# A decode block on one core: the loose rows of a weight matrix dealt anew to the transfer engines

## The chip, the cores and the metric

The kernel runs on one core of one Trainium2 chip. Times are microseconds of the device; the time of a kernel is the median of its runs. In the profile PE is the matrix engine (TensorE), PEld its weight load, DVE the vector engine, ACT the scalar engine, POOL is GpSimd, and SP (SyncE) computes nothing and issues transfers. The core's transfers (DMA) run on 16 transfer engines, numbered from 0.

## The reference

One decode step of a transformer block with adaptive layer norm, for two sequences (B = 2), one token each, width 512, all in float32:

```
mod = (silu(c) @ w_mod).reshape(2, 6, 1, 512)      # w_mod: 512 x 3072
sa, ca, ga, sb, cb, gb = mod[:, 0..5]
h = layernorm(x) * (1 + ca) + sa
q = (h @ wq) in 32 heads of 128                     # wq: 512 x 4096
p = softmax(q . k_cache * 128**-0.5)                # k_cache: 2 x 32 x 4096 x 128
x = x + ga * ((p . v_cache) @ wo)                   # wo: 4096 x 512
h = layernorm(x) * (1 + cb) + sb
f = h @ w1 + b1                                     # w1: 512 x 1376
x = x + gb * ((f * tanh(softplus(f))) @ w2)         # w2: 1376 x 512
```

K and V are 134 MB each. The last sixth of `w_mod` (columns 2560 to 3071) gives the gate gb; the change is about how its 512 rows are loaded.

## The kernel before

All inputs are laid out on the host into the order in which they are loaded. 36 loads (`stream`, L37) fill three buffers ("rooms" of 128 partitions x 64 KB) in turn; a load is issued when everything in the room three loads before has been used (`used`, L161). Loads 1 to 31 are one transfer each, of one head's K and parts of V, `wq` and `wo`. The last four are different:

- load 32: V of head 28, the last two blocks of `wo`, and the modulation's third part (`m2`);
- load 33: two transfers of 4 MB with V of heads 29 and 30;
- load 34: V of the last head, the modulation's fifth part (`m4`), and loose rows of its sixth;
- load 35: the fourth part (`m3`), `w1`, most of the sixth part (`m5`), `w2`, in seven transfers, the last with 512 columns of `w2`.

A head's K is multiplied with the query and summed on DVE (`products`, `sums`), the row maximum goes over PE (`row_max`), ACT takes the exponent (`soft_max`), PE multiplies with V (`weighted_v`). After the last head comes a tail in which PE leads: the output projection, the second layer norm, `w1`, the activation, `w2`, and the store. Matmuls named `busy` (L312, on `e` and `ident`) do work that nobody needs and keep PE occupied between steps.

**The sixth part of the modulation.** 512 rows are 384 in three blocks of 128 (`m5`), 32 that sit in an unused corner of a `w2` block, and 96 loose ones. Before, the loose ones are 4 x 20 rows (`m5p`: 20 partitions, four pieces of 512 columns side by side, so 20 rows of 8 KB) and 16 rows (`m5q`: 16 partitions of 2 KB). A tensor with fewer than 128 rows is issued by `load` as four transfers (L155), every fourth row each: `m5q` as four of four rows, `m5p` as four of five rows. The gate's matmuls (`modulation_5`, L534) take the loose pieces first (terms 0 to 4), then `m5`, then the corner.

**What sets the order.** The schedule is written by hand: an engine does its instructions in the order of the program. SyncE's queue is the list of loads. Each transfer tells of its end on one of eight semaphores (DMAHW0 to DMAHW7) which are taken in turn, so a transfer also waits, at its issue, until the one that used its semaphore eight transfers before has landed. Transfers of one queue are worked off in order on each of the 16 transfer engines; a transfer over 128 partitions uses all of them, eight rows each.

Of the kernel before, what the change touches and what calls it, by code (L numbers as in the profile page):

```python
# [8 lines left out]
F32 = mybir.dt.float32  # L9
# [4 lines left out]
P = 128  # L14
WIDTHS = (384, 384, 352, 256)
CHUNKS = [(g, j) for j in range(3) for g in range(4) if WIDTHS[g] > P * j]
STEP = 4
PIECES = (20, 20, 20, 20, 16)
WHOLE = PIECES.count(PIECES[0])
M5 = 3  # L20
REST0 = WIDTHS[2] - 2 * P
REST = 512 - P * M5 - sum(PIECES)
# [4 lines left out]
HALF = BIG // 2  # L27
SIZES = {
    "k": BIG, "v": HALF, "wq": W, "wo": W, "m01": 2 * W, "m2": W, "m3": W, "m4": W, "m5": 512 * M5,
    "m5p": 512 * WHOLE, "m5q": 512, "w1": 4 * sum(WIDTHS), "w2": 512 * len(CHUNKS),  # L30
}
OUT_STEP = 1
AHEAD = (14, 22)
# [3 lines left out]
def stream():  # L37


    order, n_v = [], 0  # L40
    for h in range(1, HEADS):
        order.append(("k", h))
        if h % HC == HC - 1 and HC < h < HEADS - 1:
            c = (h + 1) // HC
            order.append([("wq", c), ("wo", c - 2)])
        if h not in AHEAD:
            order += [("v", n_v, 0), ("v", n_v, 1)]
            n_v += 1
    order = [x if isinstance(x, list) else [x] for x in order]

    def size(x):
        return sum(SIZES[key[0]] for key in x)

    loads = [[([("m01", 0), ("wq", 0), ("wq", 1)], (4 * W,)), ([("k", 0)], (BIG,))]]
    for _ in range(1, HEADS):
        row = []
        while size(row) < ROW:
            room = ROW - size(row)
            row += order.pop(next(i for i, x in enumerate(order) if size(x) <= room))
        loads.append([(row, (ROW,))])  # L60
    last = [("v", h, i) for h in range(HEADS - 4, HEADS) for i in range(2)]
    assert order == [[key] for key in last[:2]], order
    loads += [
        [(last[:2] + [("wo", 6), ("wo", 7), ("m2", 0)], (BIG + 3 * W,))],
        [(last[2:4], (BIG,)), (last[4:6], (BIG,))],
        [([("m5q", 0)], (512,)), ([("m4", 0)] + last[6:], (W + HALF, W, W)), ([("m5p", 0)], (512 * WHOLE,))],
        [
            ([("m3", 0), ("w1", 0)], (W + 2 * sum(WIDTHS), 2 * sum(WIDTHS))),
            ([("m5", 0), ("w2", 0)], (512 * (M5 + 1), 5 * 512, 3 * 512, 512, 512)),
        ],  # L70
    ]
    return loads
# [3 lines left out]
def kernel(  # L76
# [48 lines left out]
    def take(t, keys):  # L125
        lo = 0
        for key in keys:
            kind, n = key[:2]
            part = t[:, lo : lo + SIZES[kind]]
            lo += SIZES[kind]  # L130
            if kind == "k":
                k_t[n] = part.rearrange("p (j d) -> p j d", d=DH)
            elif kind == "v":
                v_t[n, key[2]] = part.rearrange("p (c n) -> p c n", n=512)
            elif kind in ("wq", "wo"):
                (wq_t if kind == "wq" else wo_t)[n] = part.rearrange("p (k n) -> p k n", k=G)
            else:
                w_t[kind] = part.rearrange("p (k n) -> p k n", k={"w2": NCH, "m5": M5, "m5p": WHOLE, "m5q": 1}.get(kind, G))

    w_t = {}  # L140
    done = set()
# [1 line left out]
    def load(n):  # L143

        t = kvp.tile([P, ROW], F32, tag="room", name=f"room{n}", bufs=3)
        lo = 0
        for keys, srcs in loads[n]:
            take(t[:, lo:], keys)
            for src in srcs:
                rows, width = src.shape  # L150
                dst = t[:rows, lo : lo + width]
                if rows == P:
                    nc.sync.dma_start(out=dst, in_=src)
                else:
                    for i in range(STEP):  # L155
                        nc.sync.dma_start(out=dst[i::STEP], in_=src[i::STEP])
                lo += width

    loaded = 0

# [42 lines left out]
    for b in range(B):  # L203
        nc.vector.memset(same[PB * b : PB * (b + 1), b, :], 1.0)
    same = same.rearrange("p b r -> p (b r)")
    eps_t = const.tile([P, 48], F32, name="eps_t")
    nc.vector.memset(eps_t, EPS)

    ct = const.tile([P, G, R], F32, name="ct")
# [316 lines left out]
    w1_t, w2_t = w_t["w1"], w_t["w2"]  # L526
    gps = ov[1 - N % 2][:, :P]
    rest5 = slice(REST0, REST0 + REST)
    wm5p = [w_t["m5p"][:, n, :] for n in range(WHOLE)] + [w_t["m5q"][:, 0, :]]
    terms5 = [(ct5[:rows, n, :], wm5p[n][:rows]) for n, rows in enumerate(PIECES)]  # L530
    terms5 += [(ct[:, k, :], wm5[:, k, :]) for k in range(M5)]
    terms5.append((ct5[rest5, len(PIECES), :], w2_t[rest5, 0, :]))

# [28 lines left out]
    h2ps = columns(hq, "h2ps")  # L562
    nc.vector.tensor_copy(h2t[:, :, ::TB], h2ps)

    busy(1)
    modulation_5(4, len(PIECES))
    hq_pad = work.tile([P, 512], F32, tag="o", name="hq_pad")
    nc.gpsimd.memset(hq_pad[:, : NJ * P], 0.0)
    w1ps = wide_ps("w1ps")
# [61 lines left out]
def _lay_out(np, a):  # L631
# [21 lines left out]
    m5 = a["w_mod"][:, 512 * 5 :]  # L653
    m5p, f0 = np.zeros((P, len(PIECES) + 1, 512), m5.dtype), P * M5
    for n, size in enumerate(PIECES + (REST,)):
        to = REST0 if n == len(PIECES) else 0
        b1c[to : to + size, 12 + 2 * n : 14 + 2 * n] = a["c"].reshape(2, 512)[:, f0 : f0 + size].T
        m5p[to : to + size, n] = m5[f0 : f0 + size]
        f0 += size
    w2 = np.zeros((P, len(CHUNKS), 512), a["B_w2"].dtype)  # L660
    for n, (g, j) in enumerate(CHUNKS):
# [3 lines left out]
        w2[: f1 - f0, (n + 1) % len(CHUNKS)] = a["B_w2"][f0:f1]  # L665
    w2[REST0 : REST0 + REST, 0] = m5p[REST0 : REST0 + REST, -1]

    pieces = {**kv, "wq": wq, "wo": wo, "m01": [wm[:, :, :1024]], "w1": [w1], "w2": [w2], "m5p": [m5p[:, :WHOLE]], "m5q": [m5p[:, WHOLE]], "m5": [rows(m5)[:, :M5]]}
    for n in (2, 3, 4):
        pieces[f"m{n}"] = [wm[:, :, 512 * n : 512 * (n + 1)]]  # L670
    def piece(kind, n, part=None):
        row = pieces[kind][n].reshape(P, -1)
        return row if part is None else row[:, HALF * part : HALF * (part + 1)]

    loose = {"m5p": PIECES[0], "m5q": PIECES[-1]}
    arrays = {
        "head": np.stack([q_rows(a["c"]), q_rows(a["A_x"])], axis=1),
        "b1c": b1c,
# [36 lines left out]
```

## Time and profile before

| | |
|---|---|
| median of three runs | 695.11 us (695.01 to 695.4) |
| profiled execution | 694.79 us, its span (first to last instruction) 693.4 us |
| busy: DVE, PE, ACT, POOL | 85%, 42%, 6%, 1% of the span |
| moved | 297.48 MB, 429 GB/s over the span |
| chain that ended last | DMA 68%, DVE 28%, PE 4% |

The span is what the profile divides up; the profiled execution's own time is 1.4 us longer. The chain of waits goes back from the last instruction to what released it. A timeline row has start, length, engine, line, instruction, tiles, count, and in brackets the engine's idle time before it and what ended it. A table of stretches has for each its length, the busy time and count of PE, PEld, DVE, ACT and POOL, PE's granted clock, the mean share of the 16 transfer engines, and GB/s.

### The profile page before, as it was taken

The numbers are of one execution on the slowest core, as the hardware profiler recorded it, in microseconds if no ns is written. First come the engines' busy times: TensorE is split into PE (matmuls) and PEld (weight loads), VectorE is DVE, ScalarE is ACT, GpSimd is POOL, SyncE is SP. The second block draws the span as 40 slices with busy tenths as digits, with TensorE's granted clock in tenths as the row PEclk, the third lists the DMA queues.
The fourth block names the chain that finished last, engine by engine and source line by source line (L and its number), as shares of the span: only waits on it lengthen the run. The fifth ranks groups of instructions, "written<-read, shape, count | busy, mean of one in ns | idle before, by whom it ended". The sixth has DMA issues, their size and how long they took to land.

```text
span 693.4 us, 4061 instructions
## 1 busy us (share of the span) xinstructions
PE 291.3 (42%) x1704; PEld 109.5 (16%) x1704; DVE 588.4 (85%) x223; ACT 44.2 (6%) x169; POOL 4.4 (1%) x20
## 2 busy tenths in 40 slices
PE   3403334335145624335232716235324426134898
PEld 1200001001012201101100301011101111001345
DVE  3799899999999999999999999999999999899102
ACT  1000000000000000000000000000000010000011
POOL 2000000000000000000000000000000000000000
PEclk9855666669565566556575565656585656656799
DMA  9999999999999999999999999999999999999997
GB/s 389 459 423 423 424 423 480 417 427 431 423 447 446 428 423 436 423 446 440 427 427 439 440 439 427 427 443 427 439 439 421 431 450 421 446 420 421 431 428 308
DMA packets 7019, 297.48 MB, mean 429 GB/s; under 512 B 941, under 2 KB 1077, under 8 KB 1477
## 3 DMA queue, kind: packets, MB, share of 16 engines
q1 hardware_dynamic: 6696, 297.14, 99.2%
q8 instruction: 13, 0.21, 0.1%
q10 hardware_dynamic: 304, 0.09, 0.1%
q14 instruction: 6, 0.04, 0.0%
HBM read 297.16 MB, written 0.07 MB: 429 GB/s over the span
## 4 chain that ended last, share of the span: by engine, by line
DMA 68%; DVE 28%; PE 4%; issue 0%; ACT 0%; SPq 0%; DVEq 0%; ACTq 0%
DMA room<-in_load 68%; DVE room L336 14%; DVE s L339 14%; PE modps L265 1%; PE ov L316 1%; PE qps L309 1%; PE yps L618 0%; PE w1ps L573 0%; PE ov L538 0%; PE ov L379 0%; PE fps L588 0%; PE otp L402 0%; DVE m L352 0%; DVE hcw L298 0%; ACT q L310 0%
## 5 line engine op out<-in xcount | busy, mean ns | idle before, releaser
L336 DVE TENSOR_TENSOR room<-room,q 128x8192 f32<-128x8192 f32 x32 | 278.2, 8692 | 45.5 <-DMA room<-in_load 41.1
L339 DVE TENSOR_REDUCE s<-room 128x64 f32<-128x8192 f32 x32 | 277.9, 8683 | 0.4 <-DVE m L352 0.3
L379 PE MATMUL ov<-room,e 128*32 128x512 f32 x1024 | 174.7, 836 | 73.0 <-ACT e L355 63.3
L348 PE MATMUL mt<-d,same 128*128 128x64 f32 x64 | 18.7, 388 | 195.7 <-DVE d L346 195.7
L379 PEld LDWEIGHTS ov<-room,e 128*32 128x32 f32 x1024 | 39.1, 145 | 178.0 <-issue 131.2
L355 ACT ACTIVATE e<-s,m 64x64 f32<-64x64 f32 x64 | 22.1, 345 | 554.3 <-DVE m L352 553.5
L348 PEld LDWEIGHTS mt<-d,same 128*128 128x128 f32 x64 | 13.5, 264 | 225.5 <-DVE d L346 180.3
L309 PE MATMUL qps<-room,hcw 128*128 128x512 f32 x64 | 42.5, 829 | 4.2 <-DMA room<-in_load 3.4
L363 PE MATMUL l<-l,ones 128*128 128x8 f32 x16 | 4.6, 358 | 74.9 <-ACT e L355 74.9
L402 PE MATMUL otp<-pick,o 128*128 128x8 f32 (+2 forms) x72 | 14.3, 326 | 34.0 <-ACT o L394 32.1
L309 PEld LDWEIGHTS qps<-room,hcw 128*128 128x128 f32 x64 | 16.5, 270 | 25.4 <-issue 20.0
L402 PEld LDWEIGHTS otp<-pick,o 128*128 128x128 f32 x72 | 13.6, 282 | 42.5 <-ACT o L394 39.8
L394 DVE COPY o<-ov 128x256 f32<-128x256 f32 x1 | 0.4, 425 | 22.9 <-ACT o L394 22.9
L363 PEld LDWEIGHTS l<-l,ones 128*128 128x128 f32 x16 | 3.8, 295 | 76.3 <-ACT e L355 76.3
L352 DVE TENSOR_REDUCE m<-mt 128x1 f32<-128x64 f32 x32 | 7.0, 217 | 6.6 <-PE mt L348 6.6
L410 PE MATMUL att<-room,ot 128*32 128x512 f32 x62 | 10.2, 719 | 5.2 <-DMA room<-in_load 4.6
L355 ACT ACTIVATION_READ_ACCUMULATOR e<-s,m 64x1 f32 x64 | 11.8, 185 | 0.0
L316 PE MATMUL ov<-e,ident 128*128 128x256 f32 (+1 forms) x44 | 11.0, 380 | 0.0
L346 DVE TENSOR_SCALAR d<-half,m 128x64 f32<-128x64 f32 x32 | 8.1, 254 | 1.1
L316 PEld LDWEIGHTS ov<-e,ident 128*128 128x128 f32 x44 | 7.6, 190 | 3.8 <-issue 3.1
L344 DVE TENSOR_REDUCE m<-s 128x1 f32<-128x64 f32 x32 | 6.9, 217 | 0.9
L265 PE MATMUL modps<-room,ct 128*32 128x128 f32 (+1 forms) x128 | 7.0, 363 | 1.2 <-DMA room<-in_load 1.2
(107 smaller groups left out, 69.5 us busy)
## 6 DMA issues: line engine op xcount, KB each, us to landing
room<-in_load SPq DMA_DIRECT2D x4, 4096.0 KB, 24.9
room<-in_load SPq DMA_DIRECT2D x1, 7168.0 KB, 39.2
room<-in_load SPq DMA_DIRECT2D x1, 3072.0 KB, 23.3
room<-in_load SPq DMA_DIRECT2D x3, 1024.0 KB, 22.0
room<-in_load SPq DMA_DIRECT2D x1, 2400.0 KB
room<-in_load SPq DMA_DIRECT2D x1, 1376.0 KB, 14.1
room<-in_load SPq DMA_DIRECT2D x1, 1280.0 KB, 14.6
room<-in_load SPq DMA_DIRECT2D x1, 768.0 KB
```

The lines of the kernel that those rows point to most:

```text
L265: nc.tensor.matmul(ps[R * g : R * (g + 1)], lhsT=ct[:, k, :], rhs=t[:, k, :].rearrange("p (m n) -> p m n", m=n)[:, :, P * g : P * (g + 1)] ...
L309: nc.tensor.matmul(ps, lhsT=hcw[:, k, :], rhs=wq_t[ch][:, k, :], start=(k == 0), stop=(k == G - 1))
L316: nc.tensor.matmul(ov[bank][:, :cols], lhsT=ident, rhs=e_t[0].rearrange("p c m -> p (c m)")[:, :cols], start=True, stop=True)
L336: nc.vector.tensor_tensor(out=k_t[h], in0=k_t[h], in1=qv, op=ALU.mult)
L339: nc.vector.tensor_reduce(out=s_t[h], in_=k_t[h], axis=AX.X, op=ALU.add)
L346: nc.vector.tensor_scalar(out=d, in0=half, scalar1=m_t[h][:, 0:1], scalar2=None, op0=ALU.mult)
L348: nc.tensor.matmul(mps[h], lhsT=same, rhs=d, start=True, stop=True)
L355: nc.scalar.activation(e_t[i][own_b, :, M * i + 4 * b : M * i + 4 * b + 4], s_t[h][own_b].rearrange("p (c m) -> p c m", m=4), AF.Exp, bias ...
L363: nc.tensor.matmul(lps[n], lhsT=ones, rhs=sum_t[n % 2], start=True, stop=True)
L379: nc.tensor.matmul(ov[bank][R * g : R * (g + 1), :], lhsT=e_t[h % HC][:, NB // 2 * part + c, :], rhs=v_t[h, part][:, c, :], start=(first a ...
L402: nc.tensor.matmul(tps[:, x], lhsT=o_t[m], rhs=pick_t[n][:, m, x], start=(m == 0), stop=(m == 3),)
L410: nc.tensor.matmul(att[R * i : R * (i + 1), :], lhsT=ot_t[n % 2][:, i, :], rhs=wo_t[n][:, i, :], start=(n == 0), stop=(n == H // HC - (2 i ...
```

## The change

All 96 loose rows become one tensor `m5p` of four pieces, 24 rows of 8 KB. They lie no longer on neighbouring partitions but in five blocks of eight (partitions 0 to 7, 8 to 15, ...), with 8, 5, 5, 3 and 3 rows used in them (`SHARES`, `PLACES`), in a tile of 40 partitions (`BLOCK`) whose unused rows are zero; GpSimd writes zeros into the whole tile before the rows are loaded. The transfers are: three of one row each (partitions 7, 6, 5: `EARLY`), put behind the first wide transfer of load 34, and five behind the other wide ones (`DEAL`): two of three rows (partitions 4, 12, 20, then 3, 11, 19) and three of five rows (2, 10, 18, 26, 34 and so on). By the change's words, the n-th row of each goes to transfer engine n, so that engines 0 to 4 get 8, 5, 5, 3, 3 rows. The gate has one loose term less (four instead of five), each over 40 partitions instead of 20; where the fifth was computed, `busy(1)` becomes `busy(3)`. `eps_t` is wider by as much as `ct5` is narrower.

```diff
-STEP = 4
-PIECES = (20, 20, 20, 20, 16)
-WHOLE = PIECES.count(PIECES[0])
+OWN = 8
+SHARES = (8, 5, 5, 3, 3)
+EARLY = [slice(j, j + 1) for j in (7, 6, 5)]
+DEAL = [slice(j, 3 * OWN, OWN) for j in (4, 3)] + [slice(j, 5 * OWN, OWN) for j in (2, 1, 0)]
+PLACES = [OWN * e + j for e, n in enumerate(SHARES) for j in range(n)]
+BLOCK = OWN * len(SHARES)
+PIECES = (len(PLACES),) * 4
+WHOLE = len(PIECES)
...
-        [([("m5q", 0)], (512,)), ([("m4", 0)] + last[6:], (W + HALF, W, W)), ([("m5p", 0)], (512 * WHOLE,))],
+        [([("m4", 0)] + last[6:], (W + HALF, W, W)), ([("m5p", 0)], (512 * WHOLE,))],
...
-        lo = 0
+        lo, parts = 0, []
         for keys, srcs in loads[n]:
             take(t[:, lo:], keys)
             for src in srcs:
                 rows, width = src.shape
                 dst = t[:rows, lo : lo + width]
+                lo += width
                 if rows == P:
-                    nc.sync.dma_start(out=dst, in_=src)
+                    parts.append((dst, src))
                 else:
-                    for i in range(STEP):
-                        nc.sync.dma_start(out=dst[i::STEP], in_=src[i::STEP])
-                lo += width
+                    nc.gpsimd.memset(dst, 0.0)
+                    parts[1:1] = [(dst[deal], src[deal]) for deal in EARLY]
+                    parts += [(dst[deal], src[deal]) for deal in DEAL]
+        for dst, src in parts:
+            nc.sync.dma_start(out=dst, in_=src)
...
-    eps_t = const.tile([P, 48], F32, name="eps_t")
+    eps_t = const.tile([P, 80], F32, name="eps_t")
...
-    wm5p = [w_t["m5p"][:, n, :] for n in range(WHOLE)] + [w_t["m5q"][:, 0, :]]
-    terms5 = [(ct5[:rows, n, :], wm5p[n][:rows]) for n, rows in enumerate(PIECES)]
+    terms5 = [(ct5[:BLOCK, n, :], w_t["m5p"][:BLOCK, n, :]) for n in range(WHOLE)]
...
-    busy(1)
-    modulation_5(4, len(PIECES))
+    busy(3)
...
-        to = REST0 if n == len(PIECES) else 0
-        b1c[to : to + size, 12 + 2 * n : 14 + 2 * n] = a["c"].reshape(2, 512)[:, f0 : f0 + size].T
-        m5p[to : to + size, n] = m5[f0 : f0 + size]
+        to = slice(REST0, REST0 + size) if n == WHOLE else PLACES
+        b1c[to, 12 + 2 * n : 14 + 2 * n] = a["c"].reshape(2, 512)[:, f0 : f0 + size].T
+        m5p[to, n] = m5[f0 : f0 + size]
...
-    loose = {"m5p": PIECES[0], "m5q": PIECES[-1]}
+    loose = {"m5p": BLOCK}
```

SyncE's queue from load 34 to the beginning of load 35, before (`room34` is the buffer of load 34, `in_load34_0_0` an input in device memory, the numbers are rows x columns of float32, and in brackets stand the semaphores awaited):

```order
L156 DMA room34_1227<-in_load34_0_0 4x512 [waits DMAHW2_49,DVE_49,PE_49]
L156 DMA room34_1227<-in_load34_0_0 4x512 x3
L153 DMA room34_1227<-in_load34_1_0 128x6144
L153 DMA room34_1227<-in_load34_1_1 128x2048 [waits DMAHW3_49]
L153 DMA room34_1227<-in_load34_1_2 128x2048 [waits DMAHW4_49]
L156 DMA room34_1227<-in_load34_2_0 5x2048 [waits DMAHW5_49]
L156 DMA room34_1227<-in_load34_2_0 5x2048 [waits DMAHW6_49]
L156 DMA room34_1227<-in_load34_2_0 5x2048 [waits DMAHW7_49]
L156 DMA room34_1227<-in_load34_2_0 5x2048 [waits DMAHW0_49]
L153 DMA room35_1361<-in_load35_0_0 128x4800 [waits DMAHW1_49,PE_49]
```

Here the first loose transfer takes the semaphore after load 33's second one (which has DMAHW5), and the four five-row ones wait for that one and for the small ones of four rows, long landed. The same place now:

```order
L165 DMA room34_1227<-in_load34_0_0 128x6144 [waits DMAHW2_49,DVE_49,PE_49]
L165 DMA room34_1227<-in_load34_1_0 1x2048 [waits Pool_49]
L165 DMA room34_1227<-in_load34_1_0 1x2048 x2
L165 DMA room34_1227<-in_load34_0_1 128x2048
L165 DMA room34_1227<-in_load34_0_2 128x2048 [waits DMAHW3_49]
L165 DMA room34_1227<-in_load34_1_0 3x2048 [waits DMAHW4_49]
L165 DMA room34_1227<-in_load34_1_0 3x2048 [waits DMAHW5_49]
L165 DMA room34_1227<-in_load34_1_0 5x2048 [waits DMAHW6_49]
L165 DMA room34_1227<-in_load34_1_0 5x2048 [waits DMAHW7_49]
L165 DMA room34_1227<-in_load34_1_0 5x2048 [waits DMAHW0_49]
L165 DMA room35_1362<-in_load35_0_0 128x4800 [waits DMAHW1_49,PE_49]
```

The wide transfer 128x6144 is now first and has DMAHW6, so the first five-row transfer waits for that wide one's landing, and load 35's first piece stands behind it. The single rows wait for GpSimd's memset of `room34` (40x2048), which itself waits until the room is free.

PE between the second layer norm and `w1`, before:

```order
L316 MATMUL ov_110<-e_160,ident 128x128
L538 MATMUL ov_109<-room_1227,ct_104 32x128 x8
L255 MATMUL h2ps<-ident,hq 128x8
L316 MATMUL ov_110<-e_160,ident 128x128
L538 MATMUL ov_109<-room_1227,ct_104 32x128 x4
L573 MATMUL w1ps<-room_1361,h2t 32x384 x2
```

After the column form of the normed input (`h2ps`) come a fill and the fifth loose term, then `w1`. Now:

```order
L324 MATMUL ov_110<-e_160,ident 128x128
L545 MATMUL ov_109<-room_1227,ct_104 32x128 x8
L263 MATMUL h2ps<-ident,hq 128x8
L324 MATMUL ov_110<-e_160,ident 128x256
L324 MATMUL ov_110<-e_160,ident 128x128
L579 MATMUL w1ps<-room_1362,h2t 32x384 x2
```

A fill of 256 columns and one of 128 stand where one of 128 columns and four matmuls of the gate stood. Everything else on PE, and the order on DVE and ACT, is as before.

More of the change, by code (lines that the diff above doesn't have):

```diff
@@ L29 @@
     "k": BIG, "v": HALF, "wq": W, "wo": W, "m01": 2 * W, "m2": W, "m3": W, "m4": W, "m5": 512 * M5,
-    "m5p": 512 * WHOLE, "m5q": 512, "w1": 4 * sum(WIDTHS), "w2": 512 * len(CHUNKS),
+    "m5p": 512 * WHOLE, "w1": 4 * sum(WIDTHS), "w2": 512 * len(CHUNKS),
 }
@@ L137, in take @@
             else:
-                w_t[kind] = part.rearrange("p (k n) -> p k n", k={"w2": NCH, "m5": M5, "m5p": WHOLE, "m5q": 1}.get(kind, G))
+                w_t[kind] = part.rearrange("p (k n) -> p k n", k={"w2": NCH, "m5": M5, "m5p": WHOLE}.get(kind, G))
     w_t = {}
@@ L666, in _lay_out @@
     w2[REST0 : REST0 + REST, 0] = m5p[REST0 : REST0 + REST, -1]
-    pieces = {**kv, "wq": wq, "wo": wo, "m01": [wm[:, :, :1024]], "w1": [w1], "w2": [w2], "m5p": [m5p[:, :WHOLE]], "m5q": [m5p[:, WHOLE]], "m5": [rows(m5)[:, :M5]]}
+    pieces = {**kv, "wq": wq, "wo": wo, "m01": [wm[:, :, :1024]], "w1": [w1], "w2": [w2], "m5p": [m5p[:, :WHOLE]], "m5": [rows(m5)[:, :M5]]}
     for n in (2, 3, 4):
```

## The prediction

> **What bounds the kernel now.** I read the page first, then the chain of waits in order of time, then the last microseconds as a timeline and as a table by stretches. The page says that the transfer engines are the resource that never rests:
>
> ```profile
> span 693.4 us, 4061 instructions
> DMA  9999999999999999999999999999999999999997
> DMA packets 7019, 297.48 MB, mean 429 GB/s; under 512 B 941, under 2 KB 1077, under 8 KB 1477
> q1 hardware_dynamic: 6696, 297.14, 99.2%
> q8 instruction: 13, 0.21, 0.1%
> ```
>
> Only the last of 40 slices falls to 7 tenths. 429 GB/s over 16 engines is 26.8 GB/s for one, so a row of 8 KB costs its engine 8192 B / 26.8 = 0.306 us. That is the price in which everything below is counted. The chain of waits, its end:
>
> ```profile
> 622.50 28.39 DMA room<-in_load
> 650.90 21.97 DMA room<-in_load
> 672.92 1.07 PE ov L379 x8
> 682.40 2.76 PE w1ps L573 x16
> 690.63 0.47 PE yps L618 x8
> ```
>
> Until 672.9 the chain is transfers: the second half of the last head's V (load 34) lands there. From there on it is TensorE work to the end, 18 us, beside which load 35 streams in. The last eight matmuls, on the last 512 columns of `w2`, show which of the two is late. Timeline (start, length, what, idle time before it):
>
> ```profile
> 688.20 2.12 PEld L618 LDWEIGHTS yps<-room,actt 96*32 96x32 f32 x80 [0.33 <-issue]
> 690.63 0.16 PEld L618 LDWEIGHTS yps<-room,actt 128*32 128x32 f32 x8 [0.30 <-DMA room<-in_load]
> ```
>
> The 80 weight loads before end at 690.32, twenty groups of four in 2.12 us, 0.11 us a group. Without a wait the last two groups would begin at 690.43. They begin at 690.63, released by a transfer. So the final transfer costs 0.20 us and no more: **whatever the change does for the transfers, it can win 0.20 us here and then TensorE is the bound**, unless the landing at 672.9 moves too. What it can lose has no such cap.
>
> How uneven the 16 engines end, by stretches (span, busy times and counts by engine, clock, DMA share, GB/s; a packet counts in the stretch in which it starts):
>
> ```profile
> 687.00:687.50 0.50, 0.50 (x20) 0.18 (x12) 0.42 (x3) 0.00 (x0) 0.00 (x0) 1.00 0.82 332
> 688.50:689.00 0.50, 0.50 (x29) 0.50 (x21) 0.00 (x0) 0.00 (x0) 0.00 (x0) 1.00 0.42 160
> 689.00:689.50 0.50, 0.50 (x28) 0.50 (x23) 0.00 (x0) 0.00 (x0) 0.00 (x0) 1.00 0.52 188
> 689.50:690.00 0.50, 0.50 (x30) 0.50 (x24) 0.00 (x0) 0.00 (x0) 0.00 (x0) 1.00 0.27 102
> 690.00:690.20 0.20, 0.20 (x17) 0.20 (x9) 0.00 (x0) 0.00 (x0) 0.00 (x0) 1.00 0.08 31
> 690.20:690.60 0.40, 0.40 (x16) 0.13 (x7) 0.00 (x0) 0.00 (x0) 0.00 (x0) 1.00 0.00 0
> ```
>
> One engine is a share of 0.06. About three engines are already dry at 687.5 (0.82 is 13 of 16), seven or eight work at 689, four after 689.5, one after 690.0. So the first engine ends some 3 us before the last, and the next ones end only some 0.3 us before the last. Two things make the engines differ: the loose rows that this change deals anew, and instruction fetches, of which each of the 13 above keeps one engine busy; the stretch from 75 to 76 us has one, 5.8% of 16 engines for 1 us, that is 0.93 us of one engine:
>
> ```profile
> q8 instruction: 1, 0.02, 5.8%
> ```
>
> **The change part by part.** *The deal.* Before, engines 0 to 3 carry four rows of 8 KB and four of 2 KB (40 KB), engine 4 four rows (32 KB). After: 64, 40, 40, 24, 24 KB. At 26.8 GB/s that is +0.92 us for engine 0, 0 for 1 and 2, -0.61 for 3, -0.31 for 4; bytes in all stay 192 KB. No view gives a packet's engine, so which of the five is last at 690.6 is not to be read. That it is one of the five is likely: their loose rows alone cost 1.2 to 1.5 us that the other eleven don't pay, half of the spread of 3 us. If it is 3 or 4, the last landing falls by 0.3 to 0.6 us until the next engines, some 0.3 us ahead, take over: about 690.3. If it is 1 or 2, nothing moves. If it is 0, the end goes up by 0.92. I take the first: a lighter last engine, the landing near 690.3, and so the full cap, **-0.20 us**; bounds -0.20 and +0.92.
>
> *TensorE's fill.* The fifth partial product (eight passes) goes, a fill of 256 and 128 columns stands for one of 128:
>
> ```profile
> 681.59 0.47 PE L316 MATMUL ov<-e,ident 128*128 128x128 f32 x2
> 681.98 0.42 PE L538 MATMUL ov<-room,ct 16*32 16x128 f32 x8
> 682.33 1.09 PE L573 MATMUL w1ps<-room,h2t 128*32 128x384 f32 x10
> 673.92 0.92 PE L316 MATMUL ov<-e,ident 128*128 128x256 f32 x4
> 674.67 0.73 PE L402 MATMUL otp<-pick,o 128*128 128x2 f32 x6
> ```
>
> Today the first `w1` matmul starts 0.74 us after the fill's start. The same fill of three blocks is in the program at 673.92, and what follows it starts 0.75 us later; the change of tile shape that follows here may add the 0.1 us by which the gaps between such groups differ. So 0 to +0.1 us on the chain that ends in `yps`; I take **+0.05**. It comes off the cap.
>
> *SyncE's order.* The queue's rows and transfers that bear on it:
>
> ```profile
> 641.80 2.66 SPq L156 DMA_DIRECT2D room<-in_load  x4
> 644.51 6.72 SPq L153 DMA_DIRECT2D room<-in_load  x3
> 660.56 2.88 SPq L156 DMA_DIRECT2D room<-in_load  x4
> 665.28 9.37 SPq L153 DMA_DIRECT2D room<-in_load  x7
> room<-in_load SPq DMA_DIRECT2D x1, 3072.0 KB, 23.3
> ```
>
> One loose issue costs 0.7 us. The wide 3072 KB transfer, issued at 644.51, lands 23.3 us later, at 667.8; today it is issued behind four loose ones, now ahead of them, at 641.8, which wins nothing, since load 33 is still being moved. The new wait is the first five-row issue: its completion semaphore is the one of that 3072 KB transfer, so it goes out at 667.8, two more follow, and **load 35's first piece, behind them, is issued at about 667.8 + 3 x 0.7 = 669.9 instead of 665.28**. From issue to first packet takes 1.0 us, by the start of the program:
>
> ```profile
> 0.73 1.87 SPq L153 DMA_DIRECT2D room<-in_load  x4
> 0.00:1.70 1.70, 0.00 (x0) 0.00 (x0) 0.12 (x1) 0.00 (x0) 1.10 (x9) 1.00 0.00 0
> ```
>
> So packets of load 35 flow from 670.9. The last engine is through with the V pieces at 672.9, the earliest, by the spread of 3 us, at some 669.9. The earliest engines idle for about 1.0 us, and they end 3 us before the last, so that costs nothing: the cover is their lead. From a lateness of 3 us on it would cost time. The V landing at 672.9 itself has only three single rows put ahead of it, on engine 0, 0.92 us against 0.31 us of the 2 KB rows that leave; it moves only if engine 0 is last there.
>
> *The memset* of 40 x 2048 on GpSimd, for which the three single rows wait. Four of 128x512 take 1.91 us, so it is some 1.9 us:
>
> ```profile
> 2.67 1.91 POOL L328 MEMSET e<- 128x512 f32 x4
> ```
>
> It can begin at 641.8, with the first issue of load 34, when the room is free. SyncE stands still until some 643.7, then issues the rows until 646, while load 33 is still in the queues (its second transfer is what SyncE awaits before the issue at 660.56). Nothing. Cover gone, it would cost its 1.9 us. The vector and scalar steps on `ct5` are two columns narrower and off the chain: nothing.
>
> **Sum.** -0.20 + 0.05 = -0.15 us. The profiled execution took 694.79 us (span 693.4), so 694.64; the median of three runs is 695.11, 0.32 above that execution, and the same shift gives **694.96 us**.
>
> **Rivals.** *The last engine isn't relieved* (it carries five rows, or is one of the eleven): the landing stays at 690.6, TensorE's +0.05 hides behind it, 695.11. For it: four engines work after 689.5, so some of the eleven are nearly as late.
>
> *Engine 0 is the late one.* It carries 24 KB more, ends 0.92 us later, and the last eight matmuls, the product and the store follow: 696.0, slower. It decides as soon as engine 0 ends less than 0.92 us before the last one today. Against it: with nothing but loose rows engine 0 would be no later than 1 to 3; only fetches tell them apart, and 13 fetches over 16 engines leave some untouched.
>
> *The rows meet other engines' streams.* If an engine's wide transfers don't write eight neighbouring partitions, the loose rows, now on partitions 0 to 34 in blocks of eight, come in at places that others fill at that time, and up to four rows then hold up one other engine, 4 x 0.306 = 1.2 us. If that one is the late one and is not itself relieved: 695.11 + 1.2 = 696.3. Nothing in this profile shows such a conflict or excludes it. The Trainium skill, DMA: Bandwidth & Descriptors, section The descriptor swizzle, speaks against the change here: it gives engine 0 the partitions 0 to 3 and 32 to 35, engine 1 4 to 7 and 36 to 39 and so on, so the old rows (four neighbours an engine) were at home and the new ones are mostly not. No view of before tests it.
>
> *The single rows are spread over all engines*, so that the change isn't the deal it says: engine 0 then carries five rows, 40 KB as before, and every engine three times 512 B more, 0.06 us. The late engine is relieved or not as above; 694.96 to 695.2. The Trainium skill, the same page, section Why a DMA increments its semaphore by 16 and not by 1, says that the row count sets the number of engines, lowest numbers first, and that a single run goes to one engine or, if it is cut up, to 16. The packet count will tell.
>
> **How the numbers follow.** Relief as forecast 0.55 (694.96; its own range 694.7 to 695.2 with the three runs' scatter of 695.01 to 695.4), no relief or a spread of single rows 0.22 (695.1), engine 0 late 0.12 (696.0), streams that meet 0.08 (to 696.3), anything else 0.03. 8 in 10: 694.5 to 696.1. A measurement of this kernel tells 0.2%, 1.39 us, from no change. No single case passes that on the slow side, 0.92 and 1.2 together do, and on the fast side the cap of 0.20 forbids it: faster 0.03, same 0.91, slower 0.06.
>
> **What would show it.** Right: the last eight `yps` loads no longer wait for a transfer, or for less than 0.30 us, and start at 690.4 to 690.55; the share after 690.0 is zero; `w1ps` starts 0 to 0.1 us later; the page counts 7019 - 16 - 20 + 24 - 12 = 6995 packets, 929 under 512 B (a transfer ends with one small packet per engine: 36 before, 3 + 6 + 15 = 24 now); load 35's first piece is issued near 669.9. Wrong: 974 or so under 512 B (rows spread), a longer wait of the last eight (engine 0 or a conflict), a V landing later than 672.9, or a DMA share clearly under 1 for all engines around 670 (the late issue not covered). The forecast falls if the total moves by more than 1 us.

## The result and the profile after

The changed kernel takes 696.17 us (median of 18 runs, 695.81 to 698.82) against 695.13 us (18 runs, 694.97 to 695.63) for the kernel before, measured together: a ratio of 1.0018 with a 95% interval of 1.0011 to 1.0026. It is slower by 1.04 us; 694.96 was forecast, and the range ended at 696.1. The profiled execution of after took 696.39 us against 694.79, so 1.60 us are to be found in the traces.

The page of after:

```profile
span 695.0 us, 4056 instructions
DMA packets 6994, 297.48 MB, mean 428 GB/s; under 512 B 928, under 2 KB 1064, under 8 KB 1448
q8 instruction: 13, 0.21, 0.1%
q14 instruction: 5, 0.04, 0.0%
```

The same bytes move in a span that is 1.6 us longer. 6995 packets and 929 under 512 B were forecast, and 974 of these if the single rows were spread over the engines. The one packet that is missing is an instruction packet on q14 (before has 6 there). So the rows are dealt as the change says.

The end of after's chain of waits (start, length, what):

```profile
644.86 28.43 DMA room<-in_load
673.30 0.33 SPq L165
675.10 17.08 DMA room<-in_load
692.22 0.47 PE yps L624 x8
```

Before, the chain went over to TensorE at 672.92 and stayed there. Now it goes from the V landing (673.29) to SyncE's issues and through another transfer until 692.18: the transfers set the end again. The timeline of after, at the steps that the prediction named (start, length, engine, line, what, and in brackets the idle time before it and what ended it):

```profile
673.33 1.06 PE L387 MATMUL ov<-room,e 128*32 128x512 f32 x8 [1.50 <-DMA room<-in_load]
680.39 1.08 PE L273 MATMUL modps<-room,ct 128*32 128x128 f32 x32 [0.56 <-DMA room<-in_load]
683.46 2.77 PE L579 MATMUL w1ps<-room,h2t 128*32 128x384 f32 x32
689.33 1.25 PEld L624 LDWEIGHTS yps<-room,actt 96*32 96x32 f32 x48 [0.33 <-issue]
690.94 0.81 PEld L624 LDWEIGHTS yps<-room,actt 128*32 128x32 f32 x32 [0.36 <-DMA room<-in_load]
692.22 0.16 PEld L624 LDWEIGHTS yps<-room,actt 128*32 128x32 f32 x8 [0.47 <-DMA room<-in_load]
```

The same rows of before:

```profile
679.34 1.08 PE L265 MATMUL modps<-room,ct 128*32 128x128 f32 x32
682.33 2.77 PE L573 MATMUL w1ps<-room,h2t 128*32 128x384 f32 x32
```

V lands 0.41 us later (673.33 against 672.92). The modulation product at 680.39 now waits 0.56 us for the first piece of load 35; before, it waited for no transfer. `yps` starts 1.13 us later (689.33 against 688.20), is stopped twice by transfers, and its last eight passes start 1.59 us later (692.22 against 690.63). That is the whole difference. All of it comes from transfers, and it begins near 670, where the table by stretches shows it. After (span, busy times and counts of PE, PEld, DVE, ACT, POOL, then clock, DMA share and GB/s):

```profile
669.00:670.00 1.00, 1.00 (x16) 0.47 (x8) 0.00 (x0) 0.00 (x0) 0.00 (x0) 1.00 0.97 410
670.00:671.00 1.00, 0.96 (x12) 0.29 (x13) 0.00 (x0) 0.00 (x0) 0.00 (x0) 1.00 1.02 366
671.00:672.00 1.00, 0.83 (x28) 0.56 (x20) 0.00 (x0) 0.00 (x0) 0.00 (x0) 1.00 0.83 230
672.00:673.00 1.00, 0.00 (x0) 0.00 (x0) 0.00 (x0) 0.00 (x0) 0.00 (x0) 1.00 1.12 365
673.00:674.00 1.00, 0.67 (x8) 0.16 (x8) 0.00 (x0) 0.00 (x0) 0.00 (x0) 1.00 0.99 343
```

Before:

```profile
670.00:671.00 1.00, 0.96 (x17) 0.29 (x12) 0.00 (x0) 0.00 (x0) 0.00 (x0) 1.00 1.19 498
671.00:672.00 1.00, 1.00 (x28) 0.57 (x20) 0.00 (x0) 0.00 (x0) 0.00 (x0) 1.00 1.02 422
672.00:673.00 1.00, 0.08 (x4) 0.08 (x8) 0.00 (x0) 0.00 (x0) 0.00 (x0) 1.00 0.98 420
673.00:674.00 1.00, 1.00 (x9) 0.16 (x9) 0.00 (x0) 0.00 (x0) 0.00 (x0) 1.00 1.03 442
```

A rate of 1 GB/s over 1 us is 1 KB (of 1000 bytes), so from 670 to 674 before moves 498 + 422 + 420 + 442 = 1782 KB and after 366 + 230 + 365 + 343 = 1304 KB. 478 KB are missing, 1.1 us at 429 GB/s. (A packet counts in the stretch in which it starts, hence shares above 1.) Two different things show in these rows: a share of 0.83 points to idle engines, while a share of 1.12 with only 365 GB/s points to engines that are busy and slow. The packet records, further below, divide the two.

SyncE's first issue of load 35, after (count, least, median and longest ns, first and last start):

```profile
L165 SPq DMA_DIRECT2D room<-in_load x2: 378/942/1507, 669.9 to 670.3; - x2
```

It goes out at 669.9, as forecast (before: 665.28). The trace's packet records, which give the start, the length and the bytes of every packet, have the first packet of load 35 at 670.90, the forecast's 670.9. What was not forecast is their speed: the first eight rows of 19,200 B take 1.07 to 1.70 us each, where before every such packet but one took 0.714 us.

So two suspects stand, one from the prediction's step on SyncE's order and one from its rival of the streams that meet: **the late issue of load 35**, and **the places** of the loose rows on partitions of other engines.

### The profile page after: what moved, and what is told of

The parts are those of the page before. It is cut to its first block, busy times and chain, and to the rows that moved or that the text cites. A ratio compares the mean times of both kernels' runs of the same rounds, so it can differ in the third digit from the quotient of the medians.

```text
span 695.0 us, 4056 instructions
## 1 busy us (share of the span) xinstructions
PE 291.4 (42%) x1698; PEld 109.1 (16%) x1698; DVE 589.7 (85%) x223; ACT 44.2 (6%) x169; POOL 6.2 (1%) x21
## 4 chain that ended last, share of the span: by engine, by line
DMA 67%; DVE 30%; PE 1%; SPq 0%; issue 0%; POOL 0%; ACT 0%; DVEq 0%; POOLq 0%
DMA room<-in_load 67%; DVE room L344 15%; DVE s L347 15%; PE qps L317 1%; PE modps L273 0%; SPq L165 0%; POOL room L161 0%; DVE m L360 0%; DVE hcw L306 0%; ACT q L318 0%; PE yps L624 0%; PE hps L263 0%; DVE y L631 0%; DVE hq L297 0%; DVE hq L296 0%
## 5 line engine op out<-in xcount | busy, mean ns | idle before, releaser
L317 PE MATMUL qps<-room,hcw 128*128 128x512 f32 x64 | 44.2, 857 | 4.5 <-DMA room<-in_load 3.7
L354 DVE TENSOR_SCALAR d<-half,m 128x64 f32<-128x64 f32 x32 | 9.6, 298 | 1.1
L161 POOL MEMSET room<- 40x2048 f32 x1 | 1.8, 1803 | 637.1 <-DVE s L347 637.1
```

The source lines that it names most:

```text
L317: nc.tensor.matmul(ps, lhsT=hcw[:, k, :], rhs=wq_t[ch][:, k, :], start=(k == 0), stop=(k == G - 1))
L354: nc.vector.tensor_scalar(out=d, in0=half, scalar1=m_t[h][:, 0:1], scalar2=None, op0=ALU.mult)
```

## The experiments

Each kernel was timed in five rounds beside the kernel before. Within one job the kernel before gave 695.06 us (the first four), 695.18 us (the next four) and 695.09 us (the last two).

### The early order with the change's places

After, with the three single rows and one transfer of three rows put ahead of the 3072 KB transfer, so that load 35's first issue awaits no late semaphore.

```diff
-                    parts[1:1] = [(dst[deal], src[deal]) for deal in EARLY]
-                    parts += [(dst[deal], src[deal]) for deal in DEAL]
+                    parts[0:0] = [(dst[deal], src[deal]) for deal in EARLY + DEAL[:1]]
+                    parts += [(dst[deal], src[deal]) for deal in DEAL[1:]]
```

> The changed kernel with one difference: the three single rows and the first three-row transfer are issued ahead of load 34's wide transfers, so that no loose transfer's semaphore is that of the 3072 KB transfer; load 35's first piece should again be issued near 665.3 us instead of 669.9. Late issue as the cause: the queue doesn't run dry, GB/s stays above 410 in each microsecond from 670 to 674, w1's first matmul is back near 682.4, time 695.0 (694.7 to 695.3). Rows on other engines' partitions as the cause: nothing much is won, 695.8 to 696.2. The heavy engine 0 as the cause: nothing is won, 696.1.

Measured: 697.83 us (696.55 to 701.39, 6 runs), ratio 1.0047 (1.0029 to 1.0065). The profile's row of the issue and two rows of its timeline:

```profile
L165 SPq DMA_DIRECT2D room<-in_load x1: 347/347/347, 664.8 to 664.8; - x1
```

```profile
674.16 1.06 PE L387 MATMUL ov<-room,e 128*32 128x512 f32 x8 [1.62 <-DMA room<-in_load]
692.39 0.16 PEld L624 LDWEIGHTS yps<-room,actt 128*32 128x32 f32 x8 [0.45 <-DMA room<-in_load]
```

Load 35 is issued five microseconds earlier than in after, and the kernel is slower than after: V lands at 674.16, 1.24 us later than before. With the early issue the engines cannot be short of packets, so the loss that is left is not the late issue's. Neither theory had this on record. The profiled execution is the fastest of the six, 1.76 us above that of before (696.55 against 694.79); what the other five lose beyond that no profile shows.

### The old kernel with the late order

Before, with the 3072 KB transfer of load 34 put ahead of the small loose ones.

```diff
...
+        if n == HEADS + 2:
+            parts = parts[4:5] + parts[:4] + parts[5:]
...
```

> The kernel before (old deal, old partitions) with one difference: load 34's 3072 KB transfer is issued ahead of the four four-row transfers, so that the second five-row transfer waits for its landing and load 35's first piece goes out near 669.9 us. Late issue as the cause: slower than before by 0.7 to 1.2 us, 695.9 to 696.3, GB/s falls under 380 around 670 to 673. Partitions or the heavy engine 0 as the cause: as before, 695.1 (694.9 to 695.3).

Measured: 696.64 us (695.3 to 699.92, 11 runs), ratio 1.0025 (1.0015 to 1.0035). The stretches:

```profile
670.00:671.00 1.00, 0.72 (x12) 0.29 (x12) 0.00 (x0) 0.00 (x0) 0.00 (x0) 1.00 0.79 320
671.00:672.00 1.00, 1.00 (x29) 0.57 (x20) 0.00 (x0) 0.00 (x0) 0.00 (x0) 1.00 1.23 329
672.00:673.00 1.00, 0.25 (x8) 0.16 (x8) 0.00 (x0) 0.00 (x0) 0.00 (x0) 1.00 0.77 321
```

The late order alone, with the old deal at the old places, costs 1.58 us by the medians, more than the 0.7 to 1.2 us on record; the profiled execution is 0.99 us above that of before (695.78 against 694.79). The share falls to 0.79 and 0.77: engines stand idle. Between the two, a share of 1.23 moves only 329 GB/s, so there are slow packets here as well. The product with the landed V still starts at 672.84; what is late is load 35, and the last `yps` passes wait for it:

```profile
690.38 0.81 PEld L621 LDWEIGHTS yps<-room,actt 128*32 128x32 f32 x32 [0.81 <-DMA room<-in_load]
691.62 0.16 PEld L621 LDWEIGHTS yps<-room,actt 128*32 128x32 f32 x8 [0.43 <-DMA room<-in_load]
```

### The change's order with other places

After, with each engine's rows on the partitions that four-row steps give it: engine e has 4e to 4e + 3 and then 32 + 4e upwards.

```diff
-EARLY = [slice(j, j + 1) for j in (7, 6, 5)]
-DEAL = [slice(j, 3 * OWN, OWN) for j in (4, 3)] + [slice(j, 5 * OWN, OWN) for j in (2, 1, 0)]
-PLACES = [OWN * e + j for e, n in enumerate(SHARES) for j in range(n)]
-BLOCK = OWN * len(SHARES)
+EARLY = [slice(p, p + 1) for p in (35, 34, 33)]
+DEAL = [slice(32, 44, 4), slice(3, 12, 4)] + [slice(j, 20, 4) for j in (2, 1, 0)]
+PLACES = [4 * e + (j if j < 4 else 28 + j) for e, n in enumerate(SHARES) for j in range(n)]
+BLOCK = 44
```

> The changed kernel with one difference: the same 8, 5, 5, 3, 3 rows lie on partitions 0 to 3 and 32 to 35 for engine 0, 4 to 7 and 36 for engine 1, and so on (four neighbours an engine, then 32 further on), order of issue as in the change. Late issue as the cause: as the change, 695.9 to 696.3, load 35's first piece at 669.9. Partitions as the cause: the loss goes, 695.0 to 695.3. If both count: 695.4 to 695.9.

Measured: 695.81 us (695.37 to 696.82, 11 runs), ratio 1.0012 (1.0004 to 1.0021). That is in the range on record for both causes. The product with V starts at 672.92 again, 0.41 us earlier than in after. In the profiles of all the kernels whose rows lie at the old places or at these it starts between 672.72 and 672.94, with one exception that is told below, and on the blocks of eight at 673.33 or later. The end is late as in the kernel above:

```profile
690.56 0.81 PEld L624 LDWEIGHTS yps<-room,actt 128*32 128x32 f32 x32 [0.83 <-DMA room<-in_load]
691.76 0.16 PEld L624 LDWEIGHTS yps<-room,actt 128*32 128x32 f32 x8 [0.39 <-DMA room<-in_load]
```

### Both mended

The early order of the first experiment and the places of the third (both diffs above).

> Both differences together: the early order and the partitions of four neighbours. Late issue or partitions, or both: no loss left, and the deal alone shows, 694.8 to 695.2 (the forecast of the prediction was 694.96). If engine 0 with eight rows is the late one: 695.8 to 696.2 in spite of both.

Measured: 694.76 us (694.62 to 695.35, 11 runs), ratio 0.9996 (0.9988 to 1.0005). Rows of the issue and of the timeline:

```profile
L165 SPq DMA_DIRECT2D room<-in_load x1: 347/347/347, 666.0 to 666.0; - x1
```

```profile
673.63 1.06 PE L387 MATMUL ov<-room,e 128*32 128x512 f32 x8 [1.04 <-DMA room<-in_load]
683.12 2.08 PEld L579 LDWEIGHTS w1ps<-room,h2t 128*32 128x32 f32 x32
689.00 2.35 PEld L624 LDWEIGHTS yps<-room,actt 96*32 96x32 f32 x88 [0.33 <-issue]
```

All 88 `yps` passes run in one piece: no transfer stops them, and TensorE sets the end, as the prediction had it for the change. With both repaired the deal itself does no harm, so engine 0 with its eight rows is not the late one. This profiled execution is the slowest of the eleven, 695.35 us, and V's product starts 0.71 us later in it than before. The delay is older than the loose rows: the transfer that stands ahead of V's in the chain of waits lands at 651.6 here and at 650.9 before, and from there to V's landing it takes 21.95 us here and 21.97 us before. The four kernels with this deal make a square, each as its difference to the kernel before of its own job:

| | loose rows on blocks of eight | loose rows on 4e.., 32 + 4e.. |
|---|---|---|
| load 35 issued at 669.9 or later | +1.04 (after) | +0.75 |
| load 35 issued at 664.8 to 666.0 | +2.77 | -0.30 |

The late issue costs 1.05 us at the good places (0.75 + 0.30), the bad places cost 3.07 us at the early issue (2.77 + 0.30). They don't add: with bad places the late issue is the better one, by 1.73 us in the medians, though only by 0.16 us in the profiled executions (696.39 against 696.55). A reading that fits, and that no run isolates: the foreign rows do harm where the queues are full, and a dry queue takes some of them out of the way. ("Foreign" rows are those on partitions that the wide transfers of another engine fill; rows on 4e.., 32 + 4e.. are "at home", for a reason that the runs below test.)

### The old deal on blocks of eight

Before, in its own order, with the five-row transfers written to partitions j, j + 8 to j + 32 of a zeroed 40-row tile.

```diff
+PLACES = [8 * e + j for e in range(5) for j in range(STEP)]
+BLOCK = 40
...
+                    step = STEP
+                    if rows == BLOCK:
+                        nc.gpsimd.memset(dst, 0.0)
+                        step = 8
                     for i in range(STEP):
-                        nc.sync.dma_start(out=dst[i::STEP], in_=src[i::STEP])
+                        nc.sync.dma_start(out=dst[i::step], in_=src[i::step])
...
```

> The kernel before (old deal of 20 rows over five engines, old order, load 35's first piece near 665.3 us) with one difference: the five-row transfers write partitions j, j+8, ... j+32 of a zeroed tile of 40 instead of j, j+4, ... j+16. If places decide, with the queues full: slower by 0.7 to 2.5 us, 695.8 to 697.6, GB/s under 400 in some microseconds between 670 and 674 though the share stays at 1. If only the new deal is at fault: 695.1 (694.9 to 695.3).

Measured: 696.3 us (696.1 to 696.97, 11 runs), ratio 1.0018 (1.0009 to 1.0027). The stretches and the row in which V's landing shows:

```profile
671.00:672.00 1.00, 1.00 (x29) 0.57 (x20) 0.00 (x0) 0.00 (x0) 0.00 (x0) 1.00 1.28 425
672.00:673.00 1.00, 0.09 (x4) 0.00 (x0) 0.00 (x0) 0.00 (x0) 0.00 (x0) 1.00 1.22 291
673.00:674.00 1.00, 0.35 (x4) 0.16 (x8) 0.00 (x0) 0.00 (x0) 0.00 (x0) 1.00 0.70 239
```

```profile
673.65 1.06 PE L385 MATMUL ov<-room,e 128*32 128x512 f32 x8 [1.56 <-DMA room<-in_load]
```

The places alone, with the old deal and the old order, cost 1.12 us; the memset that comes with them is in the mended kernel too and does no harm there. Between 671 and 673 the share is 1.2 to 1.3 and the rate falls to 291 GB/s: the engines are busy and bring less. A packet counts in the stretch in which it starts, so the 0.70 that follows need not be idle time; the packet records in the next section show none here.

### Every loose row four partitions further up

The mended kernel, each engine's rows with the same steps but on the next engine's partitions. If only neighbourhood or step mattered, nothing would change.

```diff
-EARLY = [slice(p, p + 1) for p in (35, 34, 33)]
-DEAL = [slice(32, 44, 4), slice(3, 12, 4)] + [slice(j, 20, 4) for j in (2, 1, 0)]
-PLACES = [4 * e + (j if j < 4 else 28 + j) for e, n in enumerate(SHARES) for j in range(n)]
-BLOCK = 44
+EARLY = [slice(p, p + 1) for p in (39, 38, 37)]
+DEAL = [slice(36, 48, 4), slice(7, 16, 4)] + [slice(4 + j, 24, 4) for j in (2, 1, 0)]
+PLACES = [4 + 4 * e + (j if j < 4 else 28 + j) for e, n in enumerate(SHARES) for j in range(n)]
+BLOCK = 48
```

> The corrected kernel of the run e4_both with one difference: every loose row lies four partitions further up (engine 0's on 4 to 7 and 36 to 39, and so on), stride, order and deal as in e4_both. If it matters whose partitions a row falls on: all 24 rows fall on those of the next engine, as slow as e1_order, 696.5 to 698. If what hurt was only the stride of eight (blocks of eight neighbours): as e4_both, 694.6 to 695.0.

Measured: 698.04 us (697.57 to 699.9, 5 runs), ratio 1.0044 (1.0032 to 1.0057): 3.3 us above the mended kernel by the medians of two jobs, 2.86 us above the kernel before of its own job. V's landing and two stretches:

```profile
674.95 1.12 PE L387 MATMUL ov<-room,e 128*32 128x512 f32 x8 [2.24 <-DMA room<-in_load]
```

```profile
671.00:672.00 1.00, 1.00 (x15) 0.40 (x19) 0.00 (x0) 0.00 (x0) 0.00 (x0) 1.00 1.37 339
676.00:677.00 1.00, 1.00 (x6) 0.83 (x3) 0.42 (x1) 0.37 (x1) 0.00 (x0) 0.50 1.00 422
```

V lands 1.32 us later than in the mended kernel's profile and 2.03 us later than before, with a share of 1.37 at 339 GB/s. It is whose partitions they are that counts. The profiled execution is the slowest of the five, 699.9 us, and has something else: TensorE's granted clock is 0.50 there, in the second row, where it was 1.00 in the other runs at that time. The way from V's landing to the first `yps` pass is 693.44 - 674.95 = 18.49 us, against 689.00 - 673.63 = 15.37 us in the mended kernel. So 3.1 us of that one execution belong to the clock; how much of the other four, no profile shows. What is surely the places' is the later landing of V, some 2 us.

The packet records say what the shares only suggest. Worked out from them, packets after 660 us that took longer than 0.33 us (8 KB, usually 0.309 us) or than 0.74 us (19,200 B, usually 0.714 us), the time that they took beyond the usual, over 16 engines, and the mean time from 669 to 674 us in which an engine moved nothing:

| kernel | slow 8 KB | slow 19,200 B | excess / 16 | idle / 16 |
|---|---|---|---|---|
| before | 0 | 1 | 0.03 us | 0.01 us |
| mended (early, good places) | 0 | 1 | 0.03 us | 0.01 us |
| old deal on blocks of eight | 13 | 34 | 0.99 us | 0.01 us |
| early order, blocks of eight | 20 | 31 | 1.03 us | 0.01 us |
| rows four partitions further up | 43 | 64 | 1.79 us | 0.00 us |
| after | 18 | 47 | 0.92 us | 0.44 us |
| old kernel, late order | 4 | 16 | 0.55 us | 0.47 us |
| late order, good places | 7 | 20 | 0.71 us | 0.66 us |

With the rows at home and load 35 early, packets take the usual time. With foreign rows, packets of 8 KB (the loose rows and the last V pieces, which the records don't tell apart) and the wide ones beside them are slow, and with an early issue no engine is idle: all of that loss is slow packets. A late issue, even with all rows at home, has slow packets too, which start from 670.3 on; to these its idle time comes.

The records also say which engine ends last. On one engine a packet begins 3 to 4 ns before the end of the one ahead, so the packets of load 35 can be strung into sixteen streams (two that run within some ns of each other may be mixed up). Before, fifteen of them end 11.93 us after their last row of load 35's first piece; the sixteenth breaks off at 682.69, where an instruction fetch of 16 KB begins, and ends 1.42 us later than it would by those 11.93 us. In the four kernels with foreign rows the last data come on the stream that is last with that first piece: its last row ends at 679.92 in after, against 678.35 before, and the data 11.93 us later, at 691.85 against 690.28. In the two late kernels with rows at home the fifteen end by 690.61 and 690.94; last, at 691.24 and 691.39, is the stream with the fetch. So the two causes delay different engines and the later one sets the end, which is one reason why their costs don't add.

The Trainium skill, DMA: Bandwidth & Descriptors, section The descriptor swizzle, gives engine 0 the partitions 0 to 3 and 32 to 35, engine 1 the partitions 4 to 7 and 36 to 39, and so on. The runs agree with this pattern, though no record names a packet's engine: rows put there cost nothing, the same rows one engine's places further up 3.3 us by the medians (V's landing shows 2 us of it), on blocks of eight 1.12 us (old deal) to 3.07 us (this one).

### The first issue of load 35 between early and late

The mended kernel with only the three single rows ahead of the 3072 KB transfer, so that load 35's first piece awaits that transfer's landing, with no loose issues left between.

```diff
-                    parts[0:0] = [(dst[deal], src[deal]) for deal in EARLY + DEAL[:1]]
-                    parts += [(dst[deal], src[deal]) for deal in DEAL[1:]]
+                    parts[0:0] = [(dst[deal], src[deal]) for deal in EARLY]
+                    parts += [(dst[deal], src[deal]) for deal in DEAL]
```

> The corrected kernel of e4_both with one difference: one loose transfer fewer ahead of the wide ones, so that load 35's first piece takes the semaphore of the 3072 KB transfer and goes out at its landing, near 667.9 us, instead of 666.0 (e4_both) or 670.3 (e3_places). If a queue that is refilled needs the 2.4 us from issue to full rate that the changed kernel shows: 667.9 + 2.4 = 670.3 is just before the first engine is dry, no loss, 694.6 to 695.0. If lateness costs in proportion from the start: 695.2 to 695.5, half of the 1.05 us between e3_places and e4_both.

Measured: 694.77 us (694.5 to 695.15, 11 runs), ratio 0.9994 (0.9985 to 1.0003).

```profile
L165 SPq DMA_DIRECT2D room<-in_load x1: 351/351/351, 668.0 to 668.0; - x1
```

```profile
672.87 1.06 PE L387 MATMUL ov<-room,e 128*32 128x512 f32 x8 [0.79 <-DMA room<-in_load]
682.37 2.77 PE L579 MATMUL w1ps<-room,h2t 128*32 128x384 f32 x32
688.24 2.35 PEld L624 LDWEIGHTS yps<-room,actt 96*32 96x32 f32 x88 [0.33 <-issue]
```

```profile
690.00:690.50 0.50, 0.50 (x28) 0.48 (x24) 0.00 (x0) 0.00 (x0) 0.00 (x0) 1.00 0.00 0
```

An issue 2.7 us later than before (668.0 against 665.28) costs nothing; those of the two late kernels with rows at home, at 670.1 and 670.3, cost 1.05 to 1.58 us. So the cost isn't in proportion to the lateness from the start. The packet records have load 35's first packet at 669.44 here, beside 669.53 in the kernel before: the issue comes just ahead of the first engine's running dry. No packet of data starts after 690.0; in the kernel before one engine did, and the last eight passes waited 0.30 us for it.

### A smaller fill

The fill ahead of the `w1` product has one block of 128 columns again, in the mended kernel and in the one with the middle order. Nothing of the outputs depends on it.

```diff
-    busy(3)
+    busy(1)
```

> The corrected kernel of e4_both with one difference: the useless fill ahead of w1 is one block of 128 columns (two passes) instead of 256 and 128 (four passes); nothing of the result depends on it. TensorE is the bound at the end of e4_both, so w1 starts 0.25 to 0.3 us earlier; the last transfer lands only about 0.1 us before the last eight matmuls, so 694.6 to 694.75, 0 to 0.15 us won, and the wait for a transfer is back in the last yps loads. If the transfers were not near: 694.45.

Measured with the early order: 694.75 us (694.35 to 695.1, 11 runs), ratio 0.9993 (0.9985 to 1.0002).

> Home places, three single rows ahead of the 3072 KB transfer (load 35 first issued at about 667.9), and the fill ahead of the w1 product one block instead of three, as in the kernel before less its fifth partial product. Theory (TensorE sets the end of the version with the middle order, the transfers are through earlier: its share after 690.0 was 0): the eight passes' room of some 0.5 us comes off TensorE's chain until the transfers are the bound again; the w1 product starts 9.0 us after V's landing instead of 9.5, the last eight yps loads wait for a transfer and start at 690.0 to 690.4, in all 0 to 0.4 us off the middle version, 694.4 to 694.8. Rival (the last transfer already lands with the last eight matmuls): no difference, 694.77, the wait of the last eight takes up the whole 0.5 us.

Measured with the middle order: 694.82 us (694.62 to 695.1, 11 runs), ratio 0.9996 (0.9987 to 1.0004). Beside it the middle order ran once more:

> The middle order with home places once more, beside the version with the small fill on the same chip. Theory: 0.4 us under the kernel before as in the first series, with the yps loads in one run without a transfer wait. Rival: the first series' difference was the chip's; then no difference to the kernel before.

694.8 us (694.63 to 695.29, 11 runs), ratio 0.9997 (0.9988 to 1.0006): 0.29 us under the kernel before, too little to decide between its theory and its rival. The timeline with the middle order and the smaller fill:

```profile
682.11 2.77 PE L579 MATMUL w1ps<-room,h2t 128*32 128x384 f32 x32
690.45 0.16 PEld L624 LDWEIGHTS yps<-room,actt 128*32 128x32 f32 x8 [0.35 <-DMA room<-in_load]
```

`w1` starts 682.11 - 672.94 = 9.17 us after the V landing (672.94 in this profile), against 682.37 - 672.87 = 9.50 us with the larger fill. What that wins comes back as a wait of 0.35 us for the last transfer: with this deal TensorE and the transfers end together, and a shorter fill buys nothing more. The rival was right here.

All five runs of the four mended versions are 0.27 to 0.43 us below the kernel before, and every interval reaches above 1. They beat the changed kernel by some 1.3 us; that they beat the kernel before is likely, but no single comparison proves it.

## Why the prediction was wrong, point by point

**What bounds the kernel, and the cap of 0.20 us: right, but not for this version.** In the mended kernels with the fill of 256 and 128 columns TensorE sets the end. Their 88 `yps` loads take 2.35 us in one piece; before they took 2.59 us (688.20 to 690.79) with their wait, so the wait was worth 0.24 us, near the cap of 0.20. The medians are 0.27 to 0.43 us lower, with intervals some 0.6 us to either side, too wide to tell these sizes apart.

**The deal: right.** The forecast of a relieved last engine shows in the middle order: no packet starts after 690.0, and the last passes don't wait. By the packet records the last data land at 689.96 to 690.07 in the middle order and in both versions with the smaller fill, 690.28 before. The rival of engine 0 being late falls with it, and that of spread single rows by the packet count. In the changed kernel itself this gain lay under the two losses.

**TensorE's fill: right.** `w1` starts 9.41 us after V's landing before (682.33 - 672.92), 9.49 us in the mended kernel and 9.50 us in the middle order: +0.08 to +0.09 us, forecast 0 to 0.1.

**The memset: right.** It took 1.80 us from 641.71, forecast some 1.9 from 641.8:

```profile
641.71 1.80 POOL L161 MEMSET room<- 40x2048 f32 x1 [637.14 <-DVE s L347]
```

**SyncE's order: here it failed.** The issue at 669.9 and the first packets at 670.9 came as forecast. The step that failed is the sentence after it: the earliest engines "idle for about 1.0 us, and they end 3 us before the last, so that costs nothing". It costs 1.05 us (good places) to 1.58 us (old kernel). Two things were wrong in it.

The lead isn't free. It is there: strung together, the streams turn to load 35 between 669.53 and 672.66 before, and those without a fetch end between 687.15 and 690.28, in nearly the same order. But the stream that turns at 670.88 takes the instruction fetch at 682.69 and ends at 689.92, 0.36 us before the last. The prediction saw the fetches, and that the next engines end only some 0.3 us before the last, and still lent the 3 us of the first engine to all that are early. In the two late kernels with rows at home it is the stream with the fetch that ends last.

And the price of a dry queue was taken to be the idle time alone. That stream turns 0.38 us (old kernel) and 0.53 us (good places) later than before, but its eight rows of the first piece then take 6.37 and 6.63 us instead of 5.69 us: 0.68 and 0.94 us, more than the later turn. In the changed kernel the first eight rows of load 35 are as slow, 1.07 to 1.70 us instead of 0.714 us. In these two kernels the first packet of load 35 comes at 671.19 and 671.28, 1.7 us later than before (669.53); that already costs, far below the 3 us that the prediction named as the point from which it would.

**The streams that meet: the rival with a chance of 0.08 was true.** The Trainium skill, DMA: Bandwidth & Descriptors, section The descriptor swizzle, was beside it in the prediction and spoke against the change; with no row of before for it or against it, it got a small chance. In size the rival's 1.2 us, four rows on one other engine, is near what the old deal's places cost (1.12 us), but by luck: it isn't one engine that waits for four rows. The wide packets beside them are slowed too, 31 to 64 of 128, and V's landing moves with them, for which the prediction had named only engine 0.

**The sum.** The forecast was -0.15 us; its two terms, -0.20 and +0.05, show in the traces of the mended kernels as -0.24 and +0.08 to +0.09. Against that stands what the two causes cost together in the change as it is, 1.04 + 0.30 = 1.3 us. They can't be divided: removing the bad places alone wins 0.29 us (1.04 to 0.75, with intervals that overlap), removing the late order alone loses 1.73 us. The range ended at 696.1, below the 696.3 that the rival of the streams gave by itself, because that rival had a chance of 0.08; and the late issue, put at nothing, was in none of the cases.

## What to carry to other kernels

Rows dealt to chosen engines must also be written to those engines' own partitions, in the pattern of the wide transfers that run beside them: measure it by moving the rows one engine's places on. When an edit changes which semaphore an issue takes, work out from the time at which the first engine runs dry, in that very stage, how late the issue may be; ask what the early engines still have to do later, an instruction fetch for one, before their lead is counted as cover; and price a dry queue above its idle time. Where two causes may act, undo both as well as each: undoing one alone made this kernel slower and would have cleared the guilty one.

## What the runs showed of the hardware

- Beside rows that are written to partitions which another engine fills, 13 to 43 packets of 8 KB took 0.33 to 0.81 us instead of 0.309 us, and rows of 19,200 B up to 1.7 us instead of 0.714 us, with no engine idle when the issue was early. With rows at home and an early or middle issue at most one 8 KB packet was slow.
- Around a queue that has run dry packets are slow even with every row at home: in the two late kernels with good places, the first six or eight of load 35 took 1.2 to 1.85 us instead of 0.714 us, and a few of 8 KB ahead of them were slow too. What slows them stays open.
- An instruction fetch of 16 KB took 0.96 us at 682.69 before and 0.93 and 0.97 us at that place in the two late kernels with rows at home; the stream of the engine on which it fell ended 1.42, 1.68 and 1.42 us later than by its rows alone.
- The granted clock of TensorE fell to 0.50 from about 676 to 682 in one profiled execution, after TensorE had stood still for 2.24 us. The other kernels stood still for up to 1.62 us at that place and kept 1.00. Whether the pause is the cause, and whether the same makes the wide scatter of the slow versions (up to 701.39 us), was not tried.
